# A state-space convolution with a gated feed-forward block: one ring of four PSUM banks, gates folded into kernel magnitudes, and a new written-out order

## The chip, the core and the metric

The kernel runs on one core of a Trainium2 chip. The metric is the device time of one execution in microseconds; three runs of the kernel before took 944.83, 946.70 and 949.02 us (median 946.7). The core's engines are PE (TensorE, matmuls), DVE (VectorE), ACT (ScalarE), POOL (GpSimd) and SP (SyncE, which issues the DMAs). Each engine takes its own instructions strictly in the order in which they were written, and waits where a semaphore makes it.

## The reference

The input is 2048 tokens of 640 channels. Cut to what matters here:

```python
mod = (_silu(c) @ w_mod).reshape(c.shape[0], 6, 1, -1)
sa, ca, ga, sb, cb, gb = (mod[:, k] for k in range(6))
h = _layernorm(x, axis=-1) * (1 + ca) + sa
# A: K = 2 Re(C . exp(A dt l)), then a causal convolution by FFT, plus a skip
x = x + ga * (irfft(rfft(h) * rfft(K)) + h * D_skip)
h = _layernorm(x, axis=-1) * (1 + cb) + sb
x = x + gb * ((silu(h @ w1) * (h @ w3)) @ w2)
```

Per channel, `ga * conv(h)` is linear in `h`, and `h` is `xhat * (1 + ca) + sa`, with `xhat` the normalised input. So the factor `(1 + ca) * ga` may stand at the input, as it does before, or at the convolution kernel and the skip weight, if the shift `sa` is divided by `(1 + ca)`.

## The kernel before, in words

**Two parts.** The first part makes the convolution and lasts to about 365 us; the second is the feed-forward block (`ffn`, `pair_up`, `pair_down`), a long run of matmuls. The change touches only the first.

**The first part** takes the 640 channels in five blocks of 128 (`b` from 0 to 4, names like `g2.3.m0`: block 2, chunk 3). For each block:

- `gen_tasks`: the convolution kernel is generated in eight chunks `c` of 16 channels. POOL adds two phase tables into a tile `ph` (`g.ph`) and multiplies three magnitude tiles (`g.z0`, `g.z1` into `yy`, `g.z2` into `xx`); ACT takes the sines into PSUM tiles `tr` (`g.s0` to `g.s4`); DVE multiplies magnitudes by sines (`g.m0` to `g.m4`, tiles `yy<-yy,tr` and `xx<-tr,xx`); PE sums them with the skip weights `dsk` into `kps` (`g.p`); ACT copies that out (`g.r`, tile `ks`). Each of `ph`, `xx` and `yy` has two buffers, `tr` three banks.
- `h_tasks`: the input is loaded once more for this block (`h.l`, tile `xq`), normalised into a PSUM bank (`h.n`, tile `hn`, by ACT or DVE), multiplied on DVE by a row `rA = (1 + ca) * ga` (`h.x`, `hn<-hn,rw`), shifted on DVE by a row `rB` (`h.a`, `hb<-hn,rw`) and stored (`h.o`).
- `first_tasks`, `spectra_tasks`: matmuls take both to the frequency domain (tiles `ps`, copied to `sp`; then `fh` and `fk`); DVE multiplies the spectra (`fp<-fk,hq`, `fk<-fk,hq`, `fp<-fp,fk`); matmuls go back (`fz`), the result is copied (`zt`) and stored in DRAM (`zd`).

**Ahead of it** (`early_tasks`, `param_tasks`): SP loads parameters, four tiles `xs` of the input (16 transfers) and five blocks of modulation weights; ACT sums the rows of each input tile (`su`), DVE makes means (`mean`), ACT sums squares (`sq`); `hscale` makes the layer norm's scale. Five matmuls (`mr`) make the modulation rows in PSUM; `m` copies them to SBUF; four matmuls spread them over 128 partitions (`pr`), ACT copies six pieces (`rw`), and two DVE instructions over 640 columns make `rA` and `rB` (`fold`, `rw<-rw,wb`). The magnitudes `mag` of a block go into its exponentials with one product of 128x512 (`mag0` to `mag4`, `e<-e,mag`).

**What sets the order.** `Plan.add` collects tasks with the engines that may do them; `Plan.run` issues them in the written-out list `ORDER`, where a letter after a number picks the engine (a: ACT, d: DVE, p: POOL). `InOrder` (line 146, the line of nearly every instruction of the first part in the profile) ties each instruction to the one before it on its engine. Nothing moves at run time.

**PSUM.** Eight banks: three for `tr`, one for `kps`, three in a ring of tag `f`, one with tag `x`. The modulation matmuls hold `x`. `pbank` deals out these four by a counter, so most tasks that use it wait in the list until the modulation columns are done (`colsf`) and the first six chunks of block 0 are through.

Of the kernel before, what the change touches and what calls it, by code (L numbers as in the profile page):

```python
# [18 lines left out]
P = 128  # L19
# [15 lines left out]
1 2 3 78 4 80 5 6 81 19 14 82 20 41 84 21 7 15 83 42 8 22 153d 9 13 16 154 43 17 23 10 44 24 18 93 25 28 45 89 59 30 26 29 46 31  # L35
35 91 39 47 27 48 87 96 49 36 100 33 156 61 98 50 109 37 157 34 60 107 32 158 105 111 51 102 113 95 52 88 104 90 53 62 108 72 74
70 76 38 40 159p 160 155d 85 161 103 162 114 116 54 115 170 55 174 117 186 97 118 94 119 171 79 112 86 120 56 99 172 57 121 175
179 187 176 313 58 177 180 173 64 106 182 190 188 11 67 298 181 178 189 191 183 122 66 192 196 308 65 193 202 197 195 194 184 68
110 303 199 63 101 123 206 203 69 71 92 138 419d 207 12 185 124 208 140 198 205 142 127 204 125 200 209 163 128 420 218 132 166d
213 164 144 212 221 211 421d 214 165 167 219 168 169 75 73 77 126 134 135 129 130 133 139 210 314d 222 131 309a 227 141 136 304a  # L40
215 234 310 216 315 223 311 224 220 143 316 312 217 237 305 299a 339 228 422 306 229 335 307 225 146 226 317 238 145 231 235 201
300 336a 250 239 230 337 240 245 232 241 301 236 242 243 302 233 251 148d 247 341 244 254 253 338d 255 246 252 256 147 266 342a
260 248 149 259 257 318 261 150 258 425d 262 267 249 270 343 340a 269 151 263 271 275 268 264 272 277 282 276 273 265 278 274
345 344a 426 279 286 283 287 346a 423 291 288 284 427 424 285 428 152 0 564 569 319 565d 321 320a 289 333 570a 292 579 566 280
294 334a 322a 829 567 436 327 290 293 281 571 331 328a 295 440 437 137 580d 347 441 439 332a 442 572 296 574 438 447 443 452 445
325 444 581 297 348a 568 446 329 326a 449 455 456 448 349 457 453 458 463 450 684p 350d 330a 830d 459 323 451 460 454 582 834
468 324d 685 831 368 461 573 462 429 351 583 465 832 370 464 369 353 484 352 371 835a 374 354 372 430 466 355 1109 469 836 356
472 432p 470 837 402 467 375 373 473 485 376 477 575a 478 471 385 377 486 479 403 839 576 386 357 433 488 378 431 474 577 359
379 578 434 489 408 493 475 487 435 494 358 391 490 480 687 476 360 840a 584 481 833 361 482 500 495 491 841 392 585 496 586 409
690p 587 504 501 380 1359 842 492 503 505 509 1110a 497 502 362 498 381d 516 506 1111 382 363 838 510 499 1099 507 511 691 483  # L50
517 1112 383a 508 364d 598 686p 520 512 843 1360a 596 1113 518 513 366d 514 532 597a 1361 1364 599a 526 387 521 1362 1100a 519
525 602 388 533 527 404 536 844 688 1101 603a 389 515 534 590 522 1102 535 390 537 600 591a 405 692 523 543 594 601a 689 406 524
542 538 588 548 529 693 595a 528 592 845a 541 949p 530 589d 539 846 1094 552 544 410 549 593a 540 639 847 551 531 553 1363 407
848 701 411 633 1365a 1103 545 559 546 640 1104 550 1366 705 412 554 667 694 557 634 558 849 555 393 413 668 560 556 702 616 394
704 850 1367 851 395 365 703 673 1095a 706 561 617 717 711 707 562 710 674 712 656 547 708 396 695 721 713 610 718 709 657 1096
720 722 852 622 367 714 611a 1374 719 723 1097 650 726 733 612a 715 727 724 728 563 725 865 729 623 697p 696 737 861 1105d 738
734 651 739 857 730 698 735 862a 742 731 740 858d 699 866d 867 749 1106 700 950 743 604 1107 868d 736 855 1108 384 605d 1098 750
606d 607 1369 745 752 856a 863 608d 751 609d 613 753 744 952 741 864d 853 754 758 615a 760 755 397 759 765 756 746 614a 761 757
618 953 854a 762 400a 624 781 619 716 401 769 620 747 732 770 625 398a 955p 621 763 766 748 1370a 626 768 414 774 627 767 771
1371 776 859 784 417a 775 772 418 782 635 415a 1372 860a 416 777 773 628 783 1368 785 778 764 956 786 636 951p 881 790 629a 787  # L60
797 637 641 792 631a 638 882 898 632 791 788 954 1373 630 642 789 652 399 801 793 813 779 899 1375a 643 887 653 957 794 798 1114
888 958 644 795 817 1376 802 800 654 904 780 803 1377 799 915 808 796 905 816 806 804 1115 645 807 916 814 655 818 809 1214p 819
658 646a 824 669 805 647 659 815 820 810 675 648a 670 959 821 660 811 671 661 921 1215 672 966 1116 676 662 677 960 678 823 967
1117 932 665a 649 822 922 962p 938 663a 825 968 664 869 666 969 826 1378 970 827 1216d 812 933 870d 982 939 1126 871d 971 975
972 1130 976 963 983 828 977 973 878 1127d 1131a 985 974 978 679 879a 984 986 979 880a 991 998 987 875 680d 988 992 980 876d 964
1002 682d 989 872 999 993 877a 683 994 1003 1124 1001 874a 1007 1000 990 1122 1009 873a 1014 1004 995 883 1008 1005 996 884 1006
1010 961 1123a 889 1125a 885 1017 981 965 900 1018 890 1019 1030 1011 1132 891 886 1012 1133a 1025 1015 1020 901 1118 997 1016
892 1021 1128 902 1119a 1033 1034 1024 906 903 1031 1023 893 1032 907 1022 1039 1129a 1046 1027 1120 894a 1026 1035 917 1036
1217 1040 908 1028 1037 1041 1121a 1042 896a 1379 1146 1047 1038 895 897 918 923 1147 1048 1043 1013 1050 909 1380 1044 1049
1051 681 924 1052 919 1152 1062 925 1180 1153 1056 1053 920 1218 1163 1181 926 1045 1063 1055 1164 1381 927 1054 1220d 1057 1064  # L70
1029 1066 1059 1065 910 1058 1067 928a 1078 930a 1073 929 1068 1072 1060 913d 1221 1069 934 1071 1222 1070 1074 1082 1079 1169
935 1219 940 1170 1075 911a 936 1186 1061 1081 912 1223 1083 937 1084 1076 1080 941 1089 1085 1140 1231 942 1187 1086 1088 1197
1077 1087 1142a 1232 1141a 1382 1203 1090 1198 914 1234 1235 1134 1091 1236 943 1233 1204 1092 1136d 1237 1247 1240 944 1238
1241 1135a 1243 1093 1239 1248 1143 947a 1242 1251 1249 1385 945a 1144d 1252 1250 1145d 1137 1253 1244 1263 1258 1389 1254 1256
1138a 1257 1255 1245 1224 1139a 1259 1267 1165 1390a 1268 1148 1166 1269 1227p 1260 1264 1387 1167 1386a 1270 1266 1272 1171
1388a 1168 1265 1274 1482 1395 948 1149 1279 1271 931 1261 1396a 1276 946 1150 1383 1273 1228 1225 1172 1393 1151 1282 1173 1391
# [95 lines left out]
class Plan:  # L172

    def __init__(self):
        self.tasks = {}
# [20 lines left out]
class K:  # L196
# [291 lines left out]
    def gen_chunk(self, d0, tabs, off, E, place):  # L488
# [27 lines left out]
        def sines(i):  # L516

            if i == 2:
                return A.activation(ab, ph, AF.Abs)
# [1376 lines left out]
```

## Time and profile before

| what | us |
|---|---|
| median of three runs | 946.7 |
| the profiled execution, its own time | 945.42 |
| span from its first to its last instruction | 943.6 |
| first part, to the first rows of the feed-forward block | about 365 |
| PE busy over the span | 848.8 (90%) |
| DVE busy over the span | 699.6 (74%) |
| DVE busy from 0 to 365 us | 326.42 |
| POOL busy from 0 to 365 us | 290.21 |
| ACT busy from 0 to 365 us | 298.58 |
| PE busy from 0 to 365 us | 281.48 |

The shares over the whole span mix two parts with different limits. So the profile is read by stretches of time, and the first part alone. An instruction's row gives its own duration; where instructions of one engine overlap at their ends, the distance between two starts is what one of them costs the engine.

### The profile page before, as it was taken

Reading aid. Unit: us, or ns where it says so; the run is one execution under the profiler, and the core shown is the slowest. Engines: PE = TensorE matmul, PEld = TensorE weight load, DVE = VectorE, ACT = ScalarE, POOL = GpSimd, SP = SyncE. Lnnn points to the kernel's source line nnn. Section 1 sums busy time; section 2 is a strip of 40 time slices with the busy share of each in tenths; the row PEclk is TensorE's granted clock in tenths of the full one; section 3 lists DMA queues with packets and bytes.
Section 4 is the critical chain, followed back from the end, with each engine's and each line's share of the span. In section 5 each row is a group of like instructions: output and inputs, shape, how many; then the busy total and the mean of one; then the engine's idle time right before and its main releaser. Section 6 shows DMA issues by size and latency. Waiting matters only on the chain.

```text
span 943.6 us, 21995 instructions
## 1 busy us (share of the span) xinstructions
PE 848.8 (90%) x8963; PEld 671.7 (71%) x8963; DVE 699.6 (74%) x1223; ACT 524.2 (56%) x900; POOL 341.3 (36%) x352
## 2 busy tenths in 40 slices
PE   1167788989989997999999999999999999999997
PEld 0035767767868752777877788888888888888875
DVE  7999999989999855467567576467568777765763
ACT  6898999989788842333333244344344434445331
POOL 1888999988999533000000000001133322200000
PEclk9998999999999997999999999999999999999999
DMA  9776554433223468965515262322132111123242
GB/s 210 236 255 166 169 139 121 105 103 92 59 71 89 130 187 238 235 176 158 157 55 150 84 166 79 112 84 71 36 79 81 51 44 48 41 83 112 74 152 82
DMA packets 124940, 112.77 MB, mean 120 GB/s; under 512 B 12328, under 2 KB 107048, under 8 KB 123560
## 3 DMA queue, kind: packets, MB, share of 16 engines
q1 hardware_dynamic: 124072, 110.46, 42.1%
q8 instruction: 70, 1.15, 0.5%
q10 hardware_dynamic: 768, 0.92, 0.4%
q14 instruction: 30, 0.25, 0.1%
HBM read 90.38 MB, written 20.97 MB: 118 GB/s over the span
## 4 chain that ended last, share of the span: by engine, by line
PE 65%; DVE 17%; ACT 7%; DMA 6%; issue 3%; POOL 1%; SPq 1%; DVEq 0%; ACTq 0%; POOLq 0%
PE p L819 17%; PE acc L1066 17%; PE gu L1029 7%; PE gu L1031 6%; PE gu L1030 6%; DVE yy L146 5%; DVE fp L146 3%; DVE xx L146 2%; DMA xs<-in_x 2%; ACT tr L146 2%; PE fz L146 2%; PE kps L146 2%; PE ps L146 2%; DVE fk L146 1%; PE fk L146 1%
## 5 line engine op out<-in xcount | busy, mean ns | idle before, releaser
L1029 PE MATMUL gu<-xh,wh 128*128 128x512 f32 x270 | 106.1, 398 | 1.6 <-ACT xh L608 1.4
L1031 PE MATMUL gu<-xh,wl 128*128 128x512 f32 x270 | 105.4, 390 | 0.0
L1030 PE MATMUL gu<-xl,wh 128*128 128x512 f32 x270 | 105.2, 389 | 0.0
L146 ACT ACTIVATE tr<-ph 128x512 f32<-128x512 int32 (+1 forms) x160 | 93.6, 601 | 11.4 <-DVE yy L146 6.9
L838 POOL TENSOR_TENSOR ws<-wp 128x256 f32<-128x256 f32 x13 | 9.6, 739 | 230.9 <-DVE x L609 116.0
L146 POOL TENSOR_TENSOR ph<-p,p 128x1024 int32<-128x1024 int32 x40 | 79.1, 1979 | 11.4 <-ACT tr L146 8.6
L146 DVE TENSOR_TENSOR yy<-yy,tr 128x512 f32<-128x512 f32 (+1 forms) x80 | 75.1, 942 | 1.1
L722 ACT ACTIVATE wh<-wr 128x640 fp32r<-128x640 f32 x51 | 35.0, 732 | 67.8 <-PE gu L1030 58.3
L819 PE MATMUL p<-x,wch 128*128 128x512 f32 x208 | 68.3, 389 | 0.0
L1029 PEld LDWEIGHTS gu<-xh,wh 128*128 128x128 f32 x270 | 50.6, 188 | 17.6 <-DVE al L609 2.1
L1031 PEld LDWEIGHTS gu<-xh,wl 128*128 128x128 f32 x270 | 50.7, 188 | 11.2 <-DVE wl L732 0.4
L146 PE MATMUL kps<-yy,xx 128*32 128x64 f32 x2560 | 48.7, 226 | 10.9 <-DVE xx L146 6.4
L1030 PEld LDWEIGHTS gu<-xl,wh 128*128 128x128 f32 x270 | 50.7, 188 | 10.2 <-DVE xl L609 0.2
L735 POOL MEMSET w2l<- 64x640 f32 x1 | 0.6, 627 | 157.1 <-PE acc L1066 157.1
L146 DVE TENSOR_TENSOR xx<-tr,xx 128x512 f32<-128x512 f32 x80 | 54.2, 679 | 1.2 <-ACT tr L146 0.7
L856 DVE TENSOR_TENSOR s<-p,s 128x512 f32<-128x512 f32 x52 | 34.7, 683 | 26.8 <-ACT s L854 22.8
L146 POOL TENSOR_TENSOR yy<-e,e 128x512 f32<-128x512 f32 x48 | 52.9, 1110 | 3.3 <-issue 1.7
L1042 ACT ACTIVATE th<-gu 128x512 f32<-128x512 f32 x26 | 15.6, 600 | 65.7 <-PE gu L1031 65.7
L146 PE MATMUL ps<-wk,xb 128*64 128x128 f32 x640 | 47.7, 297 | 4.9 <-DVE hb L146 1.9
L1044 DVE TENSOR_TENSOR a<-a,gu 128x512 f32<-128x512 f32 x26 | 17.9, 687 | 45.4 <-PE gu L1031 45.2
L146 PEld LDWEIGHTS kps<-yy,xx 128*32 128x32 f32 x2560 | 42.9, 112 | 11.7 <-issue 8.5
L146 PEld LDWEIGHTS ps<-wk,xb 128*64 128x64 f32 x640 | 42.9, 220 | 10.4 <-DVE hb L146 2.2
(378 smaller groups left out, 2378.9 us busy)
## 6 DMA issues: line engine op xcount, KB each, us to landing
wr<-in_w SPq DMA_DIRECT2D x52, 320.0 KB, 3.6
zd<-zt SPq DMA_DIRECT2D x39, 256.0 KB, 4.1
w2r<-in_w SPq DMA_DIRECT2D x26, 320.0 KB, 3.5
wp<-in_w SPq DMA_DIRECT2D x26, 320.0 KB, 3.6
wq<-in_w SPq DMA_DIRECT2D x26, 320.0 KB, 3.3
low<-zd SPq DMA_DIRECT2D x48, 160.0 KB, 5.5
xs<-in_x SPq DMA_DIRECT2D x16, 320.0 KB, 11.3
hs<-hb SPq DMA_DIRECT2D x20, 256.0 KB, 3.1
```

What stands on the lines that cost most here:

```text
L146: self.prev = self.k.order(f(*a, **kw), self.prev)
L722: self.nc.scalar.activation(wh[:, i], raw[:, i], AF.Copy)
L735: self.nc.gpsimd.memset(w2l[64:].bitcast(F32), 0.0)
L819: nc.tensor.matmul(to, t[:, o], y[:, k], start=start and k == i == 0, stop=stop and (k, i) == (n - 1, 2), skip_group_check=True)
L838: G.tensor_tensor(s[0], a21, a22, op=ALU.add)
L856: add = lambda o, bk, s: V.tensor_tensor(o, bk, s, op=ALU.add)
L1029: nc.tensor.matmul(pg, wh[:, k, :], xh[:, k, :], start=(k == 0), stop=False)
L1030: nc.tensor.matmul(pg, wh[:, k, :], xl[:, k, :], start=False, stop=False)
L1031: nc.tensor.matmul(pg, wl[:, k, :], xh[:, k, :], start=False, stop=(k == KT - 1))
L1042: nc.scalar.activation(th, gu[0], AF.Tanh, scale=0.5)
L1044: nc.vector.tensor_mul(a, a, gu[1])
L1066: nc.tensor.matmul(acc[k], *two(a, w), start=(m == 0 and i == 0), stop=(m == 12 and i == 2))
```

## The change: what it does

- **Gates.** For blocks 1 to 4 the product with `rA` leaves the input: the 16 instructions `h.x` are gone, and `h.a` follows `h.n`. In exchange `rA` is multiplied into the magnitudes (`gm`, four DVE instructions of 128x128) and the skip weights (`gd`, four DVE instructions of 32x128), once for all four blocks. Block 0 keeps its product.
- **Rows.** `fold`, the four `pr` and the six copies go. In their place stand `vp` (four small matmuls that turn the rows into columns), `vc` (eight DVE instructions on 128x5 or less, that make `(1 + ca) * ga` and `sa / (1 + ca)`), ten matmuls of 128 columns and three copies.
- **Banks.** The tags `f` and `x` become four tags `b0` to `b3`. `Plan.run` picks for each task the bank whose last reader comes earliest in the list. The tasks that had to wait for `colsf` no longer do.
- **Magnitudes.** The tiles `ph`, `yy` and `xx` of a chunk are opened when each is first written, and `z0`, `z2` no longer follow `ph`.
- **Order.** `ORDER` is new in all its lines. Some tasks change engine: on DVE stand two more `mag`, one more `al8`, three more small copies of the tables (`p<-pB`), four more copies `sp<-ps`, three fewer copies `zt<-fz` and four more instructions `hn<-xq` than before.

The instructions on DVE around the modulation rows, before: `xx`, `yy` and `tr` belong to the chunks of block 0, `rw` holds the rows.

```order
L146 SCALAR_TENSOR_TENSOR rw<-rw,wb 128x640
L146 TENSOR_TENSOR rw<-rw,wb 128x640
L146 TENSOR_TENSOR xx_404<-tr_32_594,xx_404 128x512
L146 TENSOR_TENSOR hn<-hn,rw 128x512 x2
L146 TENSOR_TENSOR hb_667<-hn,rw 128x512
L146 TENSOR_TENSOR hb_675<-hn,rw 128x512
```

Now, in the same place (`pvm` is a PSUM bank, `st_n` a small SBUF tile):

```order
L146 TENSOR_TENSOR yy_325<-yy_325,tr_16_389 128x1024
L146 TENSOR_SCALAR st_n_92<-pvm 128x5
L146 SCALAR_TENSOR_TENSOR pvm<-st_n_92 128x5
L146 TENSOR_SCALAR pvm<-pvm 128x5
L146 TENSOR_TENSOR st_n_92<-pvm,st_n_92 128x5
L146 TENSOR_TENSOR st_n_92<-st_n_92,pvm 128x5
L146 RECIPROCAL st_n_92<-st_n_92 128x5
L146 TENSOR_TENSOR st_n_92<-pvm,st_n_92 128x5
L146 TENSOR_TENSOR st_n_92<-st_n_92 128x1
```

The four products of `gm`, further down:

```order
L146 TENSOR_TENSOR xx_575<-tr_48_673,xx_575 128x512
L146 TENSOR_TENSOR xx_575<-tr_48_737,xx_575 128x512
L146 TENSOR_TENSOR mag<-mag,rw 128x128 x4
L146 TENSOR_TENSOR xx_739<-tr_64_755,xx_739 128x512
L146 TENSOR_TENSOR yy_722<-yy_722,tr_64_742 128x16x32
```

The two long instructions of `fold` are gone; eight small ones stand ahead of `hscale`, and the four products of `gm` between chunks 3 and 4 of block 0. The four of `gd` (`dsk<-dsk,rw`) stand likewise in chunk 5.

On DVE in chunk 7 of block 0, where block 1's input is first made, before:

```order
L146 TENSOR_SCALAR hn<-xq_986,rs_y_h,rs_n_h 128x128 x4
L146 TENSOR_TENSOR yy_947<-yy_947,tr_112_968 128x16x32
L146 TENSOR_TENSOR hn<-hn,rw 128x512
L146 TENSOR_TENSOR yy_947<-yy_947,tr_112_1020 128x1024
L146 TENSOR_TENSOR hb_1087<-hn,rw 128x512
```

Now, in chunk 6:

```order
L146 TENSOR_TENSOR xx_938<-tr_96_1027,xx_938 128x512
L146 TENSOR_TENSOR hb_1036<-hn,rw 128x512
L146 TENSOR_SCALAR hn<-xq_1017,rs_y_h,rs_n_h 128x128 x4
L146 TENSOR_TENSOR hb_1059<-hn,rw 128x512
L146 TENSOR_TENSOR xx_938<-tr_96_1066,xx_938 128x512
```

The product between `hn` and `hb` is gone, and the tiles come one chunk earlier.

On SP at the start, from the third input tile on, before (`xs` are the input tiles, `sp` and `wb` receive modulation weights, `wk` and `wz` are tables):

```order
L146 DMA xs_170<-in_x 32x2560 x2
L146 DMA xs_170<-in_x 32x4x640 x2
L146 DMA xs_175<-in_x 32x2560 x2
L146 DMA xs_175<-in_x 32x4x640 x2
L146 DMA sp<-in_w_mod 128x1920 x3
```

Now:

```order
L146 DMA sp<-in_w_mod 128x1920
L146 DMA xs_168<-in_x 32x2560 x2
L146 DMA xs_168<-in_x 32x4x640 x2
L146 DMA wk<-in_t_wk 128x256
L146 DMA wz<-in_t_wz 128x256
L146 DMA xs_184<-in_x 32x2560 x2
L146 DMA xs_184<-in_x 32x4x640 x2
L146 DMA sp<-in_w_mod 128x1920 x2
```

A block of weights stands ahead of the third tile (which is now the input's second quarter, whose mean is `mean1`), and two tables ahead of the fourth.

The diff, cut to its core:

```diff
-1 2 3 78 4 80 5 6 81 19 14 82 20 41 84 21 7 15 83 42 8 22 153d 9 13 16 154 43 17 23 10 44 24 18 93 25 28 45 89 59 30 26 29 46 31
+1 2 3 78 5 80 9 4 81 12 20 14 84 19 6 79 42 41 82 83 8 7 21 11 43 13 22 154d 15 23 93 44 85 10 16 87 24 17 155 25 18 45 30 61 28
...
+        def bank(key):
+            free = [-1 if k is None else max((at.get(x, 1e9) for x in self.gives.get(k, [])), default=1e9) for k in held]
+            i = free.index(min(free))
+            held[i] = key
+            return i
...
     def pbank(self, name):
-        self.banks += 1
-        if self.banks % 4 == 3:
-            return self.psx.tile([P, 512], F32, name=name, tag="x")
-        return self.psg.tile([P, 512], F32, name=name, tag="f", bufs=3)
+        return self.psg.tile([P, 512], F32, name=name, tag=f"b{self.plan.banks.pop(0)}", bufs=1)
...
-                add(n + f"z{i}", "POOL", 1.03, lambda c=c, i=i: ch[c][1](i), [n + "ph", f"exp{b}"] + ([f"mag{b}"] if i == 2 else [n + "z0"] if i else []),
+                add(n + f"z{i}", "POOL", 1.03, lambda c=c, i=i: ch[c][1](i), [f"exp{b}"] + ([f"mag{b}"] if i == 2 else [n + "z0"] if i else []),
...
-            add(n + "x", "DVE", .61, lambda i=i: self.h_mul(b, i), [n + "n", "fold"], t + .1)
-            add(n + "a", "DVE", .61, lambda i=i: self.h_add(b, i), [n + "x"], t + .2, take=[("hz", 1)], give=[(bank, n + "n")])
+            if b == 0:
+                add(n + "x", "DVE", .61, lambda i=i: self.h_mul(b, i), [n + "n"] + rows, t + .1)
+            add(n + "a", "DVE", .61, lambda i=i: self.h_add(b, i), [n + "n"] + rows if b else [n + "x"], t + .2, take=[("hz", 1)], give=[(bank, n + "n")])
...
+        def gates():
+            pv = mt[1]
+            sa, ca, ga = (pv[:, k * KT:k * KT + KT] for k in range(3))
+            z, A, B, q = pv[:, 16:16 + KT], ab[:, :KT], ab[:, KT:2 * KT], ab[:, 2 * KT:]
+            V.tensor_scalar(q, ca, 1.0, None, op0=ALU.add)
+            V.scalar_tensor_tensor(z, q, -1.0, q, op0=ALU.mult, op1=ALU.max)
+            V.tensor_scalar(z, z, 1e-18, 4e-18, op0=ALU.is_lt, op1=ALU.mult)
+            V.tensor_tensor(q, z, q, op=ALU.add)
+            V.tensor_mul(A, q, ga)
+            V.reciprocal(q, q)
+            V.tensor_mul(B, sa, q)
+            V.tensor_mul(B[:, :1], B[:, :1], A[:, :1])
...
-        def fold():
-            self.rA, self.rB = self.rows[1], self.rows[0]
-            V.scalar_tensor_tensor(self.rA, self.rA, 1.0, self.rows[2], op0=ALU.add, op1=ALU.mult)
-            V.tensor_mul(self.rB, self.rB, self.rows[2])
...
+        def gate_sizes(e):
+            m = self.mag[:, 1:].rearrange("p b (e j) -> p b e j", j=4)
+            r = self.rA[:, P:].rearrange("p (b j e) -> p b e j", j=4, e=E4)
+            for k in range(NB - 1):
+                self.eng(e).tensor_tensor(m[:, k], m[:, k], r[:, k], op=ALU.mult)
+
+        def gate_skip(e):
+            for q in range(4):
+                s = slice(32 * q, 32 * q + 32)
+                d = self.dsk[s, 1:]
+                self.eng(e).tensor_tensor(d, d, self.rA[s, P:].rearrange("p (b q e) -> p b q e", q=4, e=E4)[:, :, q], op=ALU.mult)
```

More of the change, by code (lines that the diff above doesn't have):

```diff
@@ L190, in run @@
             done.add(n)
+            at[n] = len(at)
+            self.banks = [bank(k) for k in self.takes[n]]
             if f:
@@ L1483, in first_tasks @@
         for i in range(8):
-            bank = "f2" if b == 0 and m and i < 6 else "bank"
-            later = [f"k0.{x}.m" for x in range(6)] + ["colsf"]
+            bank = "bank"
             t = W[g](b, i)
@@ L1795, in keep @@
+        self.rA, self.rB = self.rw[:, 1], self.rw[:, 0]
         def keep(g):
[L1796 to L1803 removed]
```

265 lines of the change are left out of this document (143 added, 122 removed).

## The prediction

> **What bounds the kernel now.** I read the windows first, stage by stage, because the shares over the whole span mix two parts. Each row gives the stretch in us, its length, then the busy time of PE, PEld, DVE, ACT and POOL, the clock, and the DMAs' share.
>
> ```profile
> 0.00:40.00 40.00, 4.65 (x17) 3.18 (x17) 33.09 (x75) 29.85 (x63) 16.38 (x31) 1.00 0.97 253
> 40.00:80.00 40.00, 24.81 (x336) 12.93 (x336) 38.11 (x69) 34.09 (x63) 30.52 (x33) 0.87 0.56 183
> ...
> 200.00:240.00 40.00, 37.42 (x928) 30.07 (x930) 38.27 (x62) 36.53 (x64) 35.00 (x33) 1.00 0.38 106
> ...
> 280.00:320.00 40.00, 39.15 (x997) 31.69 (x998) 38.12 (x65) 32.52 (x59) 36.65 (x35) 1.00 0.35 97
> 320.00:365.00 45.00, 38.73 (x587) 22.21 (x581) 26.05 (x55) 19.02 (x34) 18.52 (x17) 0.92 0.61 175
> 365.00:944.00 579.00, 567.32 (x2697) 456.73 (x2696) 373.16 (x647) 225.62 (x352) 51.04 (x57) 1.00 0.38 104
> ```
>
> The last row is the feed-forward block: PE works 567 of 579 us and no edit touches it. So whatever the change is worth shows in the moment at which the first part ends, near 365 us. In the first part DVE is busy for 38 of 40 us in each middle stretch, and PE comes up to 39 of 40 towards its end. POOL has 35 to 37. This is a job shop with three nearly full engines, and DVE is full longest. The waits of DVE from 100 to 330 us say what it still misses (total us, how often, the longest).
>
> ```profile
> DVE sp L146 <- PE ps L146: 3.7, 4, 1.3
> DVE fp L146 <- PE fk L146: 3.2, 4, 0.9
> DVE hn L146 <- ACT hn L146: 1.5, 1, 1.5
> DVE hn L146 <- ACT hq L146: 0.9, 1, 0.9
> DVE zt L146 <- PE fz L146: 0.6, 2, 0.3
> DVE fp L146 <- ACT hq L146: 0.3, 1, 0.3
> DVE yy L146 <- POOL yy L146: 0.2, 1, 0.2
> ```
>
> These add up to 10.4 us of 230, seven of them behind PE. I therefore make the sum on DVE: its work that goes, its work that comes, and how much of the 10.4 us closes. After the last chunk, from about 330 us, follows a tail of matmuls, products and copies whose tasks stand in nearly the same order in both lists. One more copy of block 4's last results (`zt`) is done by DVE there, at 0.6 us by the price below; I leave the tail out of the sum.
>
> **The change part by part.** The rows that price DVE's instructions, and two of POOL's (count, then busy us and mean ns of one):
>
> ```profile
> L146 DVE TENSOR_TENSOR hn<-hn,rw 128x512 f32<-128x512 f32 x20 | 13.7, 688 | 1.5 <-ACT hn L146 1.5
> L146 DVE COPY sp<-ps 128x512 f32<-128x512 f32 x20 | 13.1, 681 | 3.7 <-PE ps L146 3.7
> L146 DVE TENSOR_SCALAR hn<-xq,rs_y_h,rs_n_h 128x128 f32<-128x128 f32 x16 | 6.6, 413 | 1.3 <-ACT hq L146 0.9
> L146 DVE COPY zt<-fz 128x512 f32<-128x512 f32 x9 | 6.2, 683 | 0.6 <-PE fz L146 0.6
> L146 POOL TENSOR_TENSOR al<-al,j 128x1024 f32<-128x1024 f32 x3 | 5.9, 1963 | 0.0
> L146 DVE TENSOR_TENSOR e<-e,mag 128x512 f32<-128x512 f32 x2 | 3.8, 1898 | 0.0
> L146 DVE TENSOR_SCALAR p<-pB 128x128 int32<-128x128 int32 x3 | 2.5, 842 | 0.0
> L146 DVE TENSOR_TENSOR xs_al<-al,j 128x1024 f32<-128x1024 f32 x1 | 1.2, 1219 | 0.0
> L146 POOL TENSOR_TENSOR e<-e,mag 128x512 f32<-128x512 f32 x1 | 1.1, 1107 | 0.0
> ```
>
> The timeline of DVE around 60 to 72 us (start, duration):
>
> ```profile
> 60.13 0.18 DVE L146 SCALAR_TENSOR_TENSOR rsw<-rsw,rs_v_h 128x16 f32<-128x16 f32 x1
> 62.13 0.28 DVE L146 TENSOR_SCALAR p<-pB 128x128 int32<-128x128 int32 x1
> 62.27 0.68 DVE L146 TENSOR_TENSOR xx<-tr,xx 128x512 f32<-128x512 f32 x1
> 62.87 0.67 DVE L146 TENSOR_TENSOR yy<-yy,tr 128x512 f32<-128x512 f32 x1
> 64.06 0.68 DVE L146 TENSOR_TENSOR x_e<-x_e,mag 128x512 f32<-128x512 f32 x1
> 68.43 2.35 DVE L146 SCALAR_TENSOR_TENSOR rw<-rw,wb 128x640 f32<-128x640 f32 x1
> 70.70 1.68 DVE L146 TENSOR_TENSOR rw<-rw,wb 128x640 f32<-128x640 f32 x1
> ```
>
> And POOL's at the same time:
>
> ```profile
> 64.06 1.81 POOL L146 TENSOR_TENSOR p<-p,step 128x512 int32<-128x512 int32 x1
> 68.15 1.95 POOL L146 TENSOR_TENSOR ph<-p,p 128x1024 int32<-128x1024 int32 x1
> 70.06 1.65 POOL L146 TENSOR_TENSOR yy<-e,e 128x512 f32<-128x512 f32 x1
> ```
>
> The starts at 62.27 and 62.87 show that an instruction of 128x512 with one operand in PSUM costs DVE 0.60 us, though its row says 0.68.
>
> *What goes from DVE.* Sixteen products `hn<-hn,rw` at 0.60 are 9.6 us. The pair of `fold` runs from 68.43 to 72.38, 3.9 us. Three copies `zt` are 1.8. Together 15.3 us.
>
> *What comes for certain.* Four copies `sp` at 0.60 are 2.4; four `hn` from `xq` at 0.41 are 1.7; three small table copies at 0.84 are 2.5; `al8` of block 2 is 1.2; two more `mag` products at 1.90 are 3.8. Together 11.6 us. POOL loses at least 1.96 + 2 x 1.11 = 4.2 us of work by the same moves; ACT loses copies too. Neither sets the pace by the windows, so I count that only as room for DVE's suppliers.
>
> *What comes at an uncertain price* are sixteen new small instructions: eight in `vc`, four in `gm`, four in `gd`. `fold` shows the trouble. At 640 columns its two instructions might be thought to cost little over 0.68 each. The first ends 0.7 us after POOL's `ph` (70.10), the second 0.7 us after POOL's `yy` (71.71): each waited for the POOL instruction then running. Two tiny instructions at 43 us show it bare, DVE first and then POOL:
>
> ```profile
> 42.87 1.03 DVE L146 SCALAR_TENSOR_TENSOR sc<-st_n 128x5 f32<-128x5 f32 x1
> 43.94 1.20 DVE L146 TENSOR_SCALAR sc<-sc 128x5 f32<-128x5 f32 x1
> ```
>
> ```profile
> 42.83 1.06 POOL L146 TENSOR_TENSOR xx<-e,e 128x512 f32<-128x512 f32 x1
> 43.85 1.26 POOL L146 TENSOR_TENSOR x_e<-x_e,pB 128x512 int32<-128x512 int32 x1
> ```
>
> Five columns take 1.03 and 1.20 us, ending within 0.05 us of POOL's. By contrast `rsw` at 60.13, with one side in PSUM, takes 0.18 while POOL runs, and `x_e<-x_e,mag` at 64.06 goes first and POOL's row behind it is the long one. So an instruction with all operands in SBUF costs its own time if it finds POOL idle or comes first, and else the rest of a POOL instruction; in a run of four, POOL's next one gets in between each time. The products of `gm` and `gd` have all operands in SBUF. Low end: `gm` four at 0.28 (the 128x128 row at 62.13), 1.1, and `gd` the same; high end four at 1.2, 4.8 each. For `gm` I take 3.0, because POOL has to wait for buffers when chunk 4 begins, and for `gd` 4.0, nearer the high end. In `vc` six instructions touch PSUM or may slip through at 0.18, and two that read SBUF twice cost 1.0 each: 3.0, between 1.4 (eight at 0.18) and 3.2. Together 10.0, between 3.6 and 12.8.
>
> A page of the Trainium skill bears on this: "SBUF — State Buffer", section "Who interferes with whom", says that a DVE instruction with two SBUF inputs and a POOL instruction that reads SBUF exclude each other, and that issue order decides who blocks. By that rule the four products of `gm` and of `gd` would always contend while POOL reads SBUF; the rows above agree (1.03 and 1.20 us for five columns), and the rule strictly applied is the slower rival below.
>
> *Sum on DVE:* 11.6 + 10.0 - 15.3 = +6.3 us, with ends of -0.1 and +9.1.
>
> *The waits that close.* The products that go stood between ACT's `hn` and the store; the wait of 1.5 us on `hn` loses its place. Seven us are waits on PE; there the four named banks and the lighter ACT and POOL help, and a later DVE is waited for less. No row prices this: it lies between nothing and 9 of the 10.4 us, and I take 6.0, a little over half. A new list can also make new waits; that is why nothing is the lower end and not a rule of the sum.
>
> *The start.* DVE follows the input loads; on the chain of waits (start, duration) stand
>
> ```profile
> 9.86 11.17 DMA xs<-in_x
> 21.05 11.84 DMA xs<-in_x
> ```
>
> and ACT's sums over rows cost
>
> ```profile
> L146 ACT ACTIVATE xs<-xs 128x640 f32<-128x640 f32 x12 | 8.7, 724 | 0.1
> ```
>
> and DVE's timeline has `mean1` as
>
> ```profile
> 32.08 1.91 DVE L146 TENSOR_SCALAR st_n<-st_n 128x4 f32<-128x4 f32 x1
> ```
>
> The eighth of the 16 input transfers lands at 21.0, the sixteenth at 32.9: 1.48 us each. Now a weight block of 960 KB, three such transfers, stands ahead of the third tile: it lands at about 21.0 + 7 x 1.48 = 31.4 instead of 27. Seven sums at 0.72 follow in ACT's list up to `su13`, and `mean1` waits until 36.4. DVE meets `mean1` near 34 by my estimate: it started at 32.08 before, and one product at 1.90 now stands ahead of it. That makes a wait of 2.4 us. If the wide weight block moves faster than narrow input rows, it waits for nothing. I take 0.5, since DVE has spare instructions only behind it. The fourth tile lands later than before but is read later in DVE's list; the weights `w4` and `w3`, ahead of the small loads, cost nothing on DVE.
>
> *PE, ACT.* Four small matmuls and ten of 128 columns replace four wide ones while PE works 25 of 40 us or less (4.65 and 24.81 of 40 in the first two rows): hidden. `z0` and `z2` before `ph` are the same POOL instructions in another order.
>
> **Total:** 6.3 - 6.0 + 0.5 = +0.8 us. The profiled execution took 945.4, which becomes 946.2; it lies 1.3 under the median of 946.7, and so I forecast 947.5 for a median.
>
> **The rivals.** *DVE wins* (faster): `gm`, `gd` and `vc` find POOL idle or go first, the sum on DVE is -0.1, and nearly all waits close, -9: with the start +0.5, -8.6, which gives 938.1. For it: the rows at 60.13 and 62.13 show full speed beside POOL. Against it: POOL works 35 to 37 of 40 us.
>
> *The shared access to SBUF decides* (slower): each of the eight products waits out a POOL instruction, DVE's sum is +9.1, and the waits do not close, because most are on PE and PE, fed by DVE, comes later with it. With the start +0.5 that is +9.6, 956.3. It decides from the point where DVE's extra work exceeds the waits that close by 4.7 us. For it: both instructions of `fold`, both of `sc`, and seven of ten us waiting on PE.
>
> *PE is the bound:* from 280 to 320 us it has 39.15 of 40 us; if its own list sets the end, DVE's sum counts for nothing and the time stays at 946.7. Against it: DVE misses only 10 us and PE works only 24.81 of 40 us from 40 to 80. That the multiplies do not really go is excluded by the list: four `hn<-hn,rw` stand where twenty did.
>
> **How the numbers follow.** A measurement of this kernel tells about 0.5% from no change, here 4.7 us: 942.0 to 951.4. The forecast gets 0.33, with its own range over just that interval; PE as the bound gets 0.10, and falls in the same interval; DVE wins 0.30; the shared access 0.27. So faster 0.30, same 0.43, slower 0.27. For 8 in 10 the range takes in about two thirds of each outer case: DVE wins spreads from 934 to 942 and the slower rival from 951.4 to 961, so 936.5 to 957.5.
>
> **What would show it right or wrong.** In the profile after, from the start to the last chunk's products: DVE's busy time up by about 6 us; rows `mag<-mag,rw` and `dsk<-dsk,rw` of 0.7 to 1.2 us (0.3 would be the faster rival); DVE's waits from 100 to 330 us near 4 us (over 9 would be the slower one); `mean1` within 0.5 us of its place. The forecast falls if the first part's end moves by over 4.7 us either way, or if the stretch from its end to the last instruction changes at all.

## The result, and the profile after

The changed kernel took 952.69 us (median of five runs, 951.06 to 956.17) beside 946.70 for the kernel before: a ratio of 1.0067, interval 1.0039 to 1.0095. It is slower, by 6 us, a little beyond the half per cent that was named as the least that can be told. The forecast was 947.5 with a range from 936.5 to 957.5; so the time lies inside the range, but 1.3 us beyond the interval of the forecast's likeliest case (942.0 to 951.4), on the side that had 0.27. The profiled execution has a span of 948.8 us, 5.2 longer than that of before.

The windows of the profile after, columns as in the prediction (length, then PE, PEld, DVE, ACT, POOL, clock, DMA share, GB/s):

```profile
0.00:40.00 40.00, 4.39 (x17) 3.22 (x17) 31.24 (x75) 25.55 (x55) 9.32 (x28) 1.00 0.98 231
...
200.00:240.00 40.00, 38.39 (x1008) 29.91 (x1008) 39.05 (x66) 38.72 (x70) 38.78 (x37) 1.00 0.45 115
...
280.00:320.00 40.00, 38.64 (x914) 32.13 (x904) 38.84 (x67) 32.83 (x59) 38.50 (x36) 1.00 0.24 63
320.00:365.00 45.00, 37.36 (x614) 23.25 (x611) 25.34 (x53) 18.64 (x34) 18.25 (x17) 0.93 0.66 184
365.00:949.00 584.00, 569.22 (x2698) 457.80 (x2696) 373.58 (x649) 225.06 (x352) 51.05 (x57) 0.99 0.38 104
```

And one stretch from the start to 320 us, the kernel before first:

```profile
0.00:320.00 320.00, 242.75 (x5686) 192.72 (x5687) 300.37 (x524) 279.56 (x515) 271.69 (x279) 0.98 0.50 139
```

```profile
0.00:320.00 320.00, 246.31 (x5676) 200.65 (x5677) 301.74 (x533) 274.17 (x505) 266.28 (x273) 0.96 0.50 137
```

DVE's busy time up to 320 us rose by 1.4 us, not by 6. DVE's waits from 100 to 330 us fell from 10.4 to 5.0 us:

```profile
DVE sp L146 <- PE ps L146: 3.9, 4, 1.8
DVE xx L146 <- ACT tr L146: 0.9, 2, 0.7
DVE yy L146 <- POOL yy L146: 0.2, 1, 0.2
```

So far that is good news for the change: the last product of the last chunk on DVE (`g4.6.m4`) ended at 327.85 us, where before it ended at 329.42. The loss comes behind it. The timeline of PE has the first matmul of the feed-forward block, of before and of after:

```profile
376.19 0.98 PE L1029 MATMUL gu<-xh,wh 128*128 128x512 f32 x3 [1.41 <-ACT xh L608]
```

```profile
377.94 0.73 PE L1048 MATMUL gu<-xh,wh 128*128 128x512 f32 x2 [1.24 <-ACT xh L627]
```

From 1.57 us ahead the kernel has gone to 1.75 behind. And from there to the last instruction it needs 570.9 us (948.82 - 377.94) where before needed 567.4, although no edit touches that block. PE's waits from 400 us on show 2.6 of these 3.4 us, before first:

```profile
PE acc L1066 <- DVE w2l L1018: 0.9, 2, 0.7
```

```profile
PE acc L1085 <- DVE w2l L1037: 2.0, 4, 0.8
PE gu L1048 <- DVE x L613: 1.5, 1, 1.5
```

A wait of 1.5 us is new; it stands at 408.36, 30 us behind the block's first matmul. The chain that leads to it is one of transfers: SP's timeline has (start, duration) the last store of the first part, the first weight loads behind it, and the weights for which PE waits at 408. Before:

```profile
352.98 0.42 SPq L146 DMA_DIRECT2D zd<-ztl  x1
...
362.02 1.10 SPq L700 DMA_DIRECT2D wr<-in_w  x2
...
367.09 4.98 SPq L560 DMA_DIRECT2D x<-in_x  x8
...
395.29 3.61 SPq L705 DMA_DIRECT2D wr<-in_w  x4
```

After:

```profile
355.08 0.43 SPq L146 DMA_DIRECT2D zd<-zt  x1
...
364.10 1.26 SPq L719 DMA_DIRECT2D wr<-in_w  x2
...
367.64 8.97 SPq L579 DMA_DIRECT2D x<-in_x  x8
...
399.73 2.32 SPq L724 DMA_DIRECT2D wr<-in_w  x3
```

The last store is 2.1 us later; so are the loads behind it; the eight loads of input rows then take 9.0 us to issue in place of 5.0, because SP keeps at most eight transfers under way (the last section has the figures) and those just ahead have not landed, and the weights at the end are issued 4.4 us later. PE's first matmul was late by only 1.75 us, and so it runs into these weights: ACT and DVE split them, and the instruction on DVE for which PE waits (`x`, at 407.81) stands behind that work. In before they came just in time.

The eight small gate products are the other thing to see. DVE's row of the four products `gm`, then POOL's rows of the same time:

```profile
79.33 5.27 DVE L146 TENSOR_TENSOR mag<-mag,rw 128x128 f32<-128x128 f32 x4
```

```profile
78.87 1.07 POOL L146 TENSOR_TENSOR yy<-e,e 128x512 f32<-128x512 f32 x1
79.90 2.10 POOL L146 TENSOR_TENSOR ph<-p,p 128x1024 int32<-128x1024 int32 x1
81.96 1.23 POOL L146 TENSOR_TENSOR xx<-e,e 128x512 f32<-128x512 f32 x1
83.16 2.37 POOL L146 TENSOR_TENSOR yy<-e,e 128x512 f32<-128x512 f32 x2
```

The four products last as long as the POOL instructions beside them: one ends each time POOL changes from one to the next (79.90, 81.96, 83.16, 84.3). That is 1.37 us for a product of 128 columns. The groups of DVE that answer to the prediction's rows:

```profile
L146 DVE COPY sp<-ps 128x512 f32<-128x512 f32 x24 | 16.0, 683 | 4.7 <-PE ps L146 4.7
L146 DVE TENSOR_SCALAR hn<-xq,rs_y_h,rs_n_h 128x128 f32<-128x128 f32 x20 | 8.3, 413 | 0.5
L146 DVE TENSOR_TENSOR mag<-mag,rw 128x128 f32<-128x128 f32 x4 | 5.3, 1373 | 0.0
L146 DVE TENSOR_SCALAR p<-pB 128x128 int32<-128x128 int32 x6 | 3.9, 650 | 0.0
L146 DVE TENSOR_TENSOR e<-e,mag 128x512 f32<-128x512 f32 x3 | 3.9, 1298 | 0.0
L146 DVE TENSOR_TENSOR dsk<-dsk,rw 32x128 f32<-32x128 f32 x4 | 3.5, 882 | 0.0
L146 DVE TENSOR_TENSOR hn<-hn,rw 128x512 f32<-128x512 f32 x4 | 2.7, 696 | 0.0
L146 DVE TENSOR_TENSOR x_e<-x_e,mag 128x512 f32<-128x512 f32 x2 | 1.4, 716 | 0.0
L146 DVE TENSOR_TENSOR al<-al,j 128x1024 f32<-128x1024 f32 x1 | 1.4, 1407 | 0.0
```

### The profile page after: what moved, and what is told of

Read it like the earlier page. It is cut to its first block, busy times and chain, and to the rows that moved or that the text cites. A ratio compares the mean times of both kernels' runs of the same rounds, so it can differ in the third digit from the quotient of the medians.

```text
span 948.8 us, 22025 instructions
## 1 busy us (share of the span) xinstructions
PE 852.9 (90%) x8983; PEld 681.7 (72%) x8983; DVE 700.7 (74%) x1232; ACT 517.9 (55%) x890; POOL 335.6 (35%) x346
## 3 DMA queue, kind: packets, MB, share of 16 engines
q8 instruction: 70, 1.15, 0.5%
## 4 chain that ended last, share of the span: by engine, by line
PE 61%; DVE 11%; DMA 10%; POOL 7%; ACT 5%; issue 4%; SPq 1%; DVEq 0%; ACTq 0%; POOLq 0%
PE p L838 17%; PE acc L1085 14%; PE gu L1048 6%; PE gu L1050 6%; PE gu L1049 6%; PE ps L146 3%; DMA xs<-in_x 3%; DMA wq<-in_w 2%; DVE yy L146 2%; POOL ph L146 2%; PE fz L146 2%; DMA low<-zd 2%; POOL yy L146 2%; PE kps L146 2%; PE fk L146 2%
## 5 line engine op out<-in xcount | busy, mean ns | idle before, releaser
L146 DVE TENSOR_TENSOR yy<-yy,tr 128x512 f32<-128x512 f32 x80 | 75.7, 946 | 1.8 <-ACT tr L146 0.4
L146 PE MATMUL kps<-yy,xx 128*32 128x64 f32 x2560 | 50.2, 230 | 12.3 <-DVE xx L146 4.6
```

The lines of the kernel that those rows point to most:

```text
L146: self.prev = self.k.order(f(*a, **kw), self.prev)
```

## The experiments

Two questions follow. Is the loss made behind the chunks, in the tail and the loads (theory T, later T2), or is it DVE's sum after all (R1)? And what are the eight gate products worth? All runs are timed against the kernel before on the same chip; ratios are to it, and a difference between two experiments is that of their ratios, in us of 947. "The stretch" below is the time from the first matmul of the feed-forward block to the last instruction, in the profiled execution.

**e0: the changed kernel again** (no edit).

> The changed kernel once more, as the control for the next three. It should come out at 952.7 us, 6 us over the kernel before, as it was measured. Its profile was 5.2 us longer than that of before: at the last product of the last chunk (g4.6.m4) it was 1.57 us ahead (327.85 against 329.42), at the first matmul of the feed-forward block 1.75 us behind (377.94 against 376.19), and the rest was lost behind that (a wait of 1.51 us at 408.36 and longer waits on w2l). Theory T (the loss is made in the tail and behind it): these signs come again, each within 1 us. Rival R1 (DVE's own sum, with the eight slow small products, decides, and the one profile is an accident): the signs move, and g4.6.m4 comes out behind before's 329.42.

Measured: 953.35 us, ratio 1.0080 (1.0052 to 1.0109). The profile has the last product at 328.30, the first matmul of the block at 378.64, the wait at 408.7 with 1.15 us, and 3.3 us of waits on `w2l`. The pattern comes again: DVE ahead, the kernel behind.

**e1: the order of before in the tail.** The list from the task `change` on, arranged as in before, with all edits in:

```diff
 1477 1331 1478
-1466 1393 1431 1395a 1394a 1432 1482 1398 1438 1404 1399 1400 1415 1405
+1482 1438 1466 1393 1431 1394a 1395a 1398 1415 1399 1400 1404 1416 1401
...
```

> The changed kernel with the order of before from the release of the FFN buffers on (the last matmuls, products, copies, stores and loads of the first part); everything ahead of that as changed, all edits in. Theory T: the first matmul of the feed-forward block comes 1.5 to 3 us earlier than in the changed kernel, the wait at 408 goes, and the time falls by 3 to 6 us, to 947 to 950. Rival R1: no change, 952.7 within 1.5. A further rival R2 (the FFN stretch is slower for some other reason than what the tail hands it): the first matmul comes earlier but the stretch behind it keeps its extra 3.5 us: 950 to 951.5 with the wait at 408 still there.

Measured: 954.73 us, ratio 1.0083 (1.0065 to 1.0101): no gain. The wait at 408 was gone, as T said, but the time did not follow. Its profiled execution was late long before the tail (the last product came at 334.00), and the granted clock was 0.50 until 3.8 us into the stretch, which cost PE 1.6 us there. T in its simple form, that the order of the tail makes the loss, falls.

**e2, the mirror image:** the kernel before with the changed order from the same point on.

```diff
 1342 1493
+1486
 1481 1408 1446
-1409a 1410a 1486 1413 1430 1414 1415 1419 1431 1416 1447 1432
+1410a 1409a 1447 1413 1419 1414 1415 1430 1420 1437 1421 1431
...
```

> The mirror image: the kernel before with the changed kernel's order from the same point on (and the fourth bank rule, the old products and the old loads untouched). Theory T: 946.7 becomes 949 to 952, with the first matmul of the feed-forward block 1.5 us or more later than 376.19. Rival R1: 946.7 within 1.5. Rival R2: 946.7 to 948.5.

Measured: 947.47 us, ratio 1.0011 (1.0000 to 1.0023). The first matmul came at 378.26, and the stretch was 567.3 us, as in before. T expected 949 to 952. So the new tail costs about 1 us, 2 at most, and it does not make the longer stretch by itself.

**e3: the gate products on POOL** (tasks 136, `gm`, and 137, `gd`):

```diff
-136d
+136p
...
-137d
+137p
```

> The changed kernel with the eight small gate products (four on the magnitudes, four on the skip weights) done by POOL in place of DVE. In the changed profile they cost DVE 5.2 and 3.4 us. Rival R1 (DVE's sum decides): DVE has 8.6 us less to do, POOL some 5 more, and the time falls by 4 to 8 us. Theory T: the last product of the last chunk may come earlier, but the tail loses it again as it lost 1.6 us before; the time stays within 2 us of the changed kernel.

Measured: 946.99 us, ratio 1.0003 (0.9987 to 1.0019): the whole loss is gone, 7.3 us against the control and 6.1 against the first measurement. This is R1's result. POOL's groups for the eight products:

```profile
L146 POOL TENSOR_TENSOR mag<-mag,rw 128x128 f32<-128x128 f32 x4 | 2.0, 524 | 0.0
L146 POOL TENSOR_TENSOR dsk<-dsk,rw 32x128 f32<-32x128 f32 x4 | 1.8, 448 | 0.2
```

What cost DVE 8.8 us costs POOL 3.8. The last product on DVE came at 323.48, 5.9 us ahead of before, the first matmul of the block at 371.99, 4.2 ahead, and the end at 943.58, where before has 943.63. So a lead of six became nothing, in the tail and in the stretch (571.6 us). PE's waits from 392 us on:

```profile
PE gu L1048 <- DVE x L613: 1.9, 1, 1.9
PE acc L1085 <- DVE w2l L1037: 1.4, 3, 0.8
```

R1 is right about the price of the products, T about where a lead goes. The next runs take the two apart.

**e4: a later load of input rows**, first try, on top of e3:

```diff
-            if b == 0 and m in (2, 4):
-                self.load_x2(m // 2 + 1)
+            if b == 0 and m in (2, 6):
+                self.load_x2(2 if m == 2 else 3)
```

> The changed kernel with the eight gate products on POOL, and one edit in the feed-forward part: the load of the fourth group of input rows, which nobody reads before the tenth block of weights, is issued two blocks of weights later (at the sixth, not the fourth). With the gates on POOL the last chunk was done 5.9 us sooner than in the kernel before, and the kernel was still no faster; PE waited 1.87 us at 402.8 for weights that stood behind that load in the queue. Theory T2 (the first part's gain is handed back behind it, to the loads): the wait goes, and the time falls from 947.0 to about 945 (944 to 946). Rival R3 (the loads only look late, PE would be late anyway): 947 within 1, with the wait in another place.

Measured: 947.65 us, ratio 1.0012 (0.9997 to 1.0028), and the wait still 1.34 us. The edit missed its aim: the order of the block's loads is set by a scheduler when the program is built, and it left this one ahead of the weights. It tells nothing on T2.

**e5: no gate products at all.**

```diff
-        add("gm", ("POOL", "DVE"), (1.5, 1.0), gate_sizes, ["q1.v3"] + rows, 22, port=True)
-        add("gd", ("POOL", "DVE"), (1.5, 1.0), gate_skip, ["dsk"] + rows, 22, port=True)
+        add("gm", ("POOL", "DVE"), (1.5, 1.0), None, ["q1.v3"] + rows, 22, port=True)
+        add("gd", ("POOL", "DVE"), (1.5, 1.0), None, ["dsk"] + rows, 22, port=True)
```

> The changed kernel without the eight gate products at all (four on the magnitudes, four on the skip weights), so blocks 1 to 4 of the convolution lack their gates; everything else stays. This gives what the products cost in all. If what they cost was DVE's waiting for POOL's running instruction, the work itself being worth about 2 us on either engine, then leaving them out comes out as moving them did: 947 within 1.5. If the work is paid wherever it stands, it falls below that by the 4 to 5 us that POOL then spent: 942 to 944.

Measured: 943.97 us, ratio 0.9984 (0.9966 to 1.0002). That is 1.8 us below e3, and the intervals overlap; taken as it is, about half of POOL's 3.8 us shows. Of the 9.1 us that the products cost against the control, 7.3 were the engine that they stood on.

**e6, more on POOL:** as e3, and `al8` of block 2 and the magnitude products of blocks 2 and 3 back where before had them.

```diff
-681d
+681p
...
-683d
+683p
...
-944d
+944p
```

> The changed kernel with the gate products on POOL and, as in the kernel before, the magnitude products of blocks 2 and 3 and al8 of block 2 on POOL as well. DVE has some 2.5 us less to do, POOL 4 more. If DVE's sum decides the time (R1): 943.5 to 945.5. If POOL or what comes behind the first part holds it (T2): 946 to 949.

Measured: 945.64 us, ratio 0.9991 (0.9978 to 1.0003), 1.1 us below e3, which the intervals do not clear. The last product came at 320.58, 2.9 us earlier than in e3, and the first matmul at 370.12, 1.9 earlier; 1.2 arrived at the end. The time falls between the ranges of the two theories.

**e7: the later load alone, in the kernel before** (the edit of e4).

> The kernel before with the same later load of the fourth group of input rows. PE shows no wait near 400 there, so T2 expects no change: 947 within 1. If the queue of loads holds more of the feed-forward block's beginning than the waits show, it falls by over 1.5.

Measured: 946.82 us, ratio 0.9999 (0.9988 to 1.0011), stretch 567.4 us. No change; as e4's edit did not move the load past the weights, this is only a second profile of before's first part.

**e8: the load really behind the weights**, on top of e3, tied to a matmul of the block:

```diff
-            if b == 0 and m in (2, 4):
-                self.load_x2(m // 2 + 1)
+            if b == 0 and m in (2, 9):
+                self.load_x2(2 if m == 2 else 3, None if m == 2 else self.mm)
...
-    def load_x2(self, b):
+    def load_x2(self, b, hold=None):
         for q in range(4):
-            self.held_back(self.nc.sync.dma_start(self.x2[b][q * 32:(q + 1) * 32], self.xv[q, :, 4 * b:4 * b + 4, :]))
+            self.held_back(self.nc.sync.dma_start(self.x2[b][q * 32:(q + 1) * 32], self.xv[q, :, 4 * b:4 * b + 4, :]), hold)
...
-        self.inverse(2 * u, 2, self.zu, ps, tag, bufs, 0, D, h)
+        self.mm = self.inverse(2 * u, 2, self.zu, ps, tag, bufs, 0, D, h)
```

> As e4, but the load of the fourth group of input rows is now tied to a matmul of the feed-forward block, so that it really stands behind the weights in the queue (in e4 it had only moved from the 17th to the 25th place among the loads that begin the block, still ahead of the weights for which PE waited, which is why e4 said nothing). 1.3 MB less, about 5 us of transfers, stand before those weights. Theory T2: the wait of 1.9 us at 30 us behind the first matmul of the block goes and the time falls to about 945 (944 to 946). Rival R3 (the wait has another cause than the queue): wait and time stay, 947 within 1.

Measured: 945.67 us, ratio 0.9984 (0.9973 to 0.9995), 1.8 us below e3. PE's waits from 392 us on are one row now:

```profile
PE acc L1085 <- DVE w2l L1037: 3.3, 4, 1.1
```

The wait at 400 is gone, as T2 said: the `x` on DVE that PE waited for now starts 24.2 us behind the block's first matmul, in e3 30.2. The profiled execution (a span of 948.1 us) does not show a shorter stretch, though: a clock of 0.50 in its first 3.7 us and longer waits on `w2l` fill it to 572.9. The gain rests on the timed runs, and the intervals of e3 and e8 just overlap (by the medians alone it is 0.9 us).

**e9: the same on top of e6.**

> e6 (gate products, the magnitude products of blocks 2 and 3 and al8 of block 2 on POOL) with the same tied load. T2: 945.6 less the wait of 1.7 us, about 944, so faster than the kernel before by 0.3 per cent. R3: 945.6 within 1.

Measured: 943.32 us, ratio 0.9969 (0.9952 to 0.9985), 2.1 us below e6 (2.0 by the medians). The intervals of this pair overlap too, but the second pair agrees with the first, and this is the version that beats both kernels: it is ahead of before by 0.15 to 0.48 per cent.

**e10: PE's order at the end of the chunks.** On top of e3, the group `k4.2.m` (1390) and the copies that empty its banks ahead of the product of the last chunk but one:

```diff
 1325 1470
+1390
 1346
+1391a
 1322 1185
+1392d
...
 1474
-1390 1456
 1328 1347 1402 1329 1403 1471 1330
-1391a 1392a
```

> The changed kernel with the gate products on POOL, and near the end of the chunks one group of matmuls (k4.2.m, with the copies that empty its banks) ahead of the product of the last chunk but one, about where the kernel before has it; in the changed list it stands between the last chunk's products on DVE and the matmul that uses them. In the changed profile that matmul started 2.5 us after its last operand was ready, in before 0.4 us. If PE's own order makes the tail longer: from the last product on DVE to the first matmul of the feed-forward block 48.5 us becomes 46.5 to 47.5, and the time about 945.5. If PE waits there for its instructions to be loaded (three waits that the profile gives to nothing, 3 us in sum, each within 3 us behind a transfer of 16 KB of instructions): no change, 947 within 1, and the waits of this kind stay near 3 us.

Measured: 948.54 us, ratio 1.0021 (1.0008 to 1.0035), 1.7 us above e3. From the last product to the block's first matmul it took 46.3 us, as hoped, but the last product came 3.3 us later (326.75), and the first matmul at 373.09, 1.1 later. PE had done this work earlier, met a new wait of 1.2 us for DVE's `zt`, and two of the three waits given to "issue" went; nothing was gained. The stretch was the longest of all, 575.9 us, with a wait of 2.6 us at 402 and 3.4 us at a granted clock of 0.50 just behind it. How much of the later product is the edit's is open: e4 and e8, whose chunks are those of e3, had it at 323.81 and 325.58.

**e11, the control for e8 and e9:** the kernel before with the tied load.

> The control for e8 and e9: the kernel before, unchanged but for the tied load of the fourth group of input rows. With the gates on POOL this edit took away a wait of 1.9 us and 1.3 to 1.8 us of time. The kernel before has no wait near 400. T2 (before had the loads just in time, the changed kernel's loads start relatively later): no change, 946.7 within 1. If before falls by 1.5 us too, then e8's gain is no part of what the change lost, and the best kernel's lead over before is smaller by as much.

Measured: 946.69 us, ratio 0.9998 (0.9984 to 1.0012): no change. Before has no wait there, and loses nothing to that load.

## Why the prediction was right, and where it failed

The time lies inside the range, and the mechanism on DVE was right in kind. What was wrong are sizes in the sum on DVE, and what was left out behind it.

**What goes from DVE** was right: the four products that stay cost 2.7 us in place of 13.7, `fold` is gone, and so are three `zt` copies.

**What comes for certain** was 11.6 us in the forecast and 7.7 in the trace: copies `sp` 2.4 (four at 0.60), `hn` from `xq` 1.7, table copies 1.4, `al8` 1.4, `mag` 0.8. The term that failed most is "two more `mag` products at 1.90": that price was itself a wait for POOL (the row at 35.11 us of before, 1.83 us long, ends 0.55 behind POOL's `ph`). Five products now cost 3.9 + 1.4 = 5.3 us, three cost some 4.5 before.

**What comes at an uncertain price** was 10.0 us and came out at 12.3: `gm` 5.3 (forecast 3.0, high end 4.8), `gd` 3.5 (4.0), and the eight of `vc` 3.5 by their rows (forecast 3.0; one of them, on a single column, took 1.87). The mechanism was right, and e3 shows it. The Trainium skill, "SBUF — State Buffer", section "Who interferes with whom", says that a DVE instruction with two SBUF inputs contends with a POOL instruction that reads SBUF, and that issue order decides; the row of 5.27 us agrees.

**The sum on DVE** was +6.3 and came out at +1.4 (0 to 320 us). The terms above make +4.7; the rest is that old small instructions met POOL less often under the new order: `mean1`, which ended 0.02 us behind a `ph` of POOL, cost 1.91 before and 0.17 now, and the five of its kind (`st_n<-st_n`, 128x4) 3.9 and 0.7. The forecast repriced only what the change touches.

**The waits that close:** 6.0 forecast, 5.4 measured on the same stretch.

**The start:** 0.5 forecast. DVE waited 1.7 us for ACT's sums (`mean2` 0.86, `mean1` 0.80). `mean1` started at 36.09; the upper bound had been 36.4, and the term lay 1.2 us too low.

**The tail and the block behind** are where the forecast failed. It said that the tail stands in nearly the same order and left it out, and that "whatever the change is worth shows in the moment at which the first part ends"; its own sign of being wrong, a change of the stretch behind that moment, came. Measured, in us:

| | before | after | after again |
|---|---|---|---|
| last product of a chunk on DVE | 329.42 | 327.85 | 328.30 |
| from there to the block's first matmul | 46.8 | 50.1 | 50.3 |
| from there to the last instruction | 567.4 | 570.9 | 572.1 |

The second row: PE, not DVE, ended the first part. When DVE was done, PE was still at a group of 64 matmuls (`k4.2.m`, 1.2 us, 327.03 to 328.19) that before does ahead of the last two chunks' sums, and it had more of the waits that the profile gives to "issue", for which it shows no releaser. PE's waits of this kind from 315 to 340 us, before and after:

```profile
PE ps L146 <- issue: 0.9, 1, 0.9
```

```profile
PE kps L146 <- issue: 1.9, 2, 1.4
PE fh L146 <- issue: 1.1, 1, 1.1
```

So the rival "PE is the bound", which had 0.10, had its part: the lead of DVE was worth nothing there. In e10, which moves the group, the time in the second row was 46.3 us, where e3 has 48.5, but the kernel gained nothing by it. Taken by the block's first matmul, the first part did end about where it was forecast: 377.94 and 378.64 after, 376.19, 377.42 and 378.91 in three profiles in which before's first part is unchanged (before, e7, e11); a mean of 0.8 us later. That the forecast said +0.8 was luck: DVE was done 1.1 to 1.6 us earlier than in the profile of before, not later, and a tail 3.3 to 3.6 us longer, which the sum left out, made up for it.

The third row is the larger failure. The stretch is 567.3 to 567.5 us in before, e2, e7 and e11, and 570.7 to 575.9 in all ten profiles made from the changed kernel. The block had its loads just in time. PE's 567 of 579 us made it look like a bound that nothing ahead could move; but the loads behind the first part's last stores set its opening, and they were left out. E8 and e9 against e3 and e6 put this wait at 1.8 to 2.1 us once it is there, and e11 shows that before does not have it.

The other part lies in the last 60 us of the stretch, where the ten profiles fall 1.6 to 3.6 us further behind before, with longer waits on `w2l`, though the order of the block is the same. The traces point to loads that are hit by the loading of instructions. Of the weights (`wq`) that these waits hang on, two loads of 640 KB, whose packets begin 501 and 531 us into the stretch of before, take 2.3 to 2.6 us in each of the four profiles with the shorter stretch, and 3.2 to 4.4 us in each of the ten others. In the four, a transfer of 16,384 bytes of instructions starts 3.7 to 4.7 us behind the first packet, when the load is done; in the ten it starts between 0.8 us ahead of that packet and 2.1 us behind it. The second load, from 907.4 us of before and from 911.2 of after, 4.2 us each (busy share of the DMA engines in tenths), and the row of the instructions that only after has there:

```profile
DMA  0008977496799999999986521000000000000000
```

```profile
DMA  0098795666988998799985412000000000100000
q8 instruction: 1, 0.02, 2.8%
```

The waits follow the loads: where the first takes 3.2 to 3.6 us (after, e1, e3, e4) PE loses nothing on `w2l` behind it by 516 us of before's stretch, where it takes 4.2 to 4.4 (e5, e6, e8, e10) 0.8 to 0.9. PE has 20 matmuls and 20 weight loads more in the changed kernel (8983 of each, 8963 before), all ahead of the block, so the 16 KB pieces of its list would end elsewhere in the block. That is argued: none of the runs moves these transfers alone.

**The slower rival** had the right mechanism by half. Moving the products off DVE takes the whole loss back, so the shared access is what made the change a loss. But it was to show as a later first part with the waits left open. Against e3 the block's first matmul is indeed 6.0 to 6.7 us later; against before, the closed waits and the cheaper small instructions make up for nearly all of that, and most of what is lost is lost in the stretch. Why 8.8 us less on DVE brings the last product only 4.4 to 4.8 us forward has part of an answer in the trace: other DVE instructions then met POOL, the three `al8` at 6.2 us in place of 3.8.

## What to carry to other kernels

Before folding a factor into tables, ask which engine multiplies them and who shares its memory access: eight small products cost one engine 8.8 us and the other 3.8. When a first part is priced by its fullest engine, follow the last stores too, and the loads that queue behind them: a block that is 98 per cent busy may have its inputs just in time, and then it gives back what the part ahead wins and adds what its transfers lose. A longer list of instructions ahead may also move the moments at which the code of an untouched stretch is loaded. And a price that is read from a row with a neighbour's wait in it is not the price of the work.

## What the runs showed of the hardware

**The same list runs differently from run to run.** DVE's `al8` of block 1, of the changed kernel and of e1, which are the same instructions up to there:

```profile
54.16 1.22 DVE L146 TENSOR_TENSOR xs_al<-al,j 128x1024 f32<-128x1024 f32 x1
```

```profile
54.76 2.91 DVE L146 TENSOR_TENSOR xs_al<-al,j 128x1024 f32<-128x1024 f32 x1
```

and POOL's instruction at the same time, in the same order:

```profile
54.16 3.02 POOL L146 TENSOR_TENSOR ph<-p,p 128x1024 int32<-128x1024 int32 x1
```

```profile
54.65 1.95 POOL L146 TENSOR_TENSOR ph<-p,p 128x1024 int32<-128x1024 int32 x1
```

Where DVE was first, POOL took 3.02 us; where POOL was first by 0.11 us, DVE took 2.91. The last product of the chunks came at 327.85, 328.30 and 334.00 us in after, e0 and e1, whose instructions are the same up to there; that such throws make up this difference is likely and not shown.

**Instructions have to be loaded.** Each of PE's 73 waits of over 0.4 us that the fourteen profiles give to "issue" ended 1.6 to 3.6 us behind the start of a transfer of 16,384 bytes of instructions; the longest was 3.3 us (e4, at 171). They come where many small matmuls follow each other without another wait. The Trainium skill, "Advanced Engine Details and Errata", section "ISA Cache", gives lines of 16 KB, 256 instructions; the size agrees. Loads of data were slower beside them: of the 140 loads of 640 KB that stand alone in the feed-forward blocks, the 20 with one under way took 3.2 to 4.4 us, the other 120 took 2.2 to 3.4.

**SP has at most eight transfers under way.** Near 379 us of before, four issues in a row came 0.01 to 0.02 us behind the landing of the eighth transfer ahead of each. In the fourteen profiles no issue began ahead of that landing, where the landing is known. So a crowd delays the loads behind it: the eight of input rows took 9.0 us to issue in the changed kernel, 5.0 before.

**The clock changes in steps.** In ten of fourteen profiles the granted clock fell to 0.50 for 3.41 or 6.83 us, beginning 3.0 to 5.4 us ahead of the block's first matmul. Where that reached into the block (e1, e8, e9), PE was about 1.6 us later after the first 5 us.
